# A mixing and gated feed-forward kernel: unit kinds in a table, priorities by tile, and two operations on GpSimd from one copy

## The chip, the cores and the metric

The kernel runs on one core of a Trainium2 chip. The metric is the device time of one execution in microseconds (us); lower is better. A profile is one execution recorded by the hardware profiler; its span goes from the first to the last instruction.

## The reference

```python
X = np.fft.fft(x, axis=1)              # x: 8 x 3008 x 256, float32
X = np.fft.fft(X, axis=2)
x = X.real.reshape(24064, 256)
g = x @ w_gate                         # 256 x 1536
silu = g * (1.0 / (1.0 + np.exp(-g)))
val = x @ w_val                        # 256 x 1536
out = (silu * val) @ w_out             # 1536 x 256
```

A real two-dimensional transform of eight sequences is followed by a gated feed-forward block over all 24064 tokens.

## The kernel before

**Symmetry.** The real part of the transform of a real sequence at position k and at the mirrored position is P + Q and P - Q, with an even part P and an odd part Q. So the kernel computes P and Q for half of the positions (12032 columns and 8 of their own) and gets two tokens from every column: a plus token and a minus (mirrored) token. The transform over the 256 features is put into the weights: `Wp` and `Wq` are the gate (index 0) and value (index 1) weights times cosine and sine tables, and `Wm` is `Wq` with the sign turned and doubled, so that adding `Wm` times Q to a finished P + Q in PSUM makes P - Q.

**Tiles and units.** The columns are cut into 24 tiles, of 512 columns but for tiles 0 and 3 (480) and 23 (320, and the 8 last columns). The 1536 hidden features are cut into 12 blocks f of 128. A unit is one pair (tile, f), 288 in all, 12 to a tile. A unit makes the hidden values `hp` (plus) and `hm` (minus) of its block; when a tile is done, `OWork` (L1188) multiplies them by `Wo`, 12 matmuls of 256 columns to each block of 128 tokens, with `psO` as target, one eviction `ev` on ScalarE (L1220) to two blocks, and stores on SP's queue (L1226). These 96 output matmuls of a tile are spread over the next tile's units.

**Kinds of units.** A plain unit adds P and Q parts of the gate in PSUM (`g`, L974, reached through `mm`), takes silu on ScalarE into `sp` (L1072), adds `Wm` to get the minus gate and takes silu of that into `sv` (L1144): three gate matmuls. The value has two: after the first, the even part is kept in `es`, and after the second the plus value stands in `v`; the mirrored value is twice `es` minus `v`, made by VectorE into `sv` (`mirror_value`, L1158). VectorE makes `hp` = `sp` x `v` (`product_p`, L1168), GpSimd makes `hm` for two units at once from `sv` (`product_m`, L1165). Variations:
- whole units (tiles 0 to 2, `whole_a` and `whole_b`): three matmuls each for gate and value, no `es`;
- seeded units (`seeded`, L957): ScalarE writes the first row's share of the value into PSUM beforehand (`seed_op`, L1046), and `es` is a plain copy on ScalarE (L1095) in place of a VectorE operation (L1097);
- gate-split units (`gate_split`, L967): two gate matmuls in place of three; VectorE keeps the even gate `sg` (L1076) and makes the mirrored gate (`mirror_gate`, L1136); the silus are L1141 and L1144;
- units on GpSimd (`on_pool`, L962): ScalarE copies `v` to `sg` (L1174), and GpSimd makes `hp` from it (`product_g`, L1177).

Which unit is which follows from lists (`SPLIT_1` to `GATE_END`, L944 to L952), one for two alternating tiles (3 to 20) and one for tiles 21 to 23.

**Transforms.** GpSimd folds the loaded x rows (`fold_step`), and a transform on TensorE (`transform_op`, two for each of eight sequences, even and odd parts apart) makes P and Q columns that VectorE puts together (L1387) in tiles from the pool `pq`, five pairs. A part of the folded rows goes to `St` from the pool `st` (three buffers) by copies on SP's queue (`spread_op`, L1339). Row 0 of Q is spread over all partitions by two DMAs on SP's queue to each tile (`br`, L1512, and `bc`, L1520).

**Order.** After a start that is written out by hand, every operation is entered in a planner, `Sched`, with its engine, a duration by formula, what it reads and writes, and the buffers that it needs. `add` (L794) gives it a place `at`: the sum of PE's planned durations so far plus a shift by its kind (`SH_ROW` to `SH_PUT`, L748 to L770). `run` (L825) then picks on each engine, among the operations whose place is at most a window (`WINDOW`, L779) behind the first one's, the one that can start first by the plan; a buffer is handed out in the order of the entries (`ready`, L851). SP's window is 6 us. The operations are issued in that order, and each engine and queue then runs its own in order, with semaphores between them.

Once, ScalarE scales the value half of `Wm` by -0.5 (L1568, at unit `FIRST + 2` = 38), after which seeded units can use it. The weights of feature blocks 4 to 11 land late; the planner has their arrival as entries with a due time (L1542 to L1544), 0 us for the first and 6 us for the second group, gate and value alike. Their products are `weight_op` (L1418).

## Time and profile before

| What | us |
|---|---|
| runs of the kernel (three) | 604.84, 605.88, 608.5; median 605.88 |
| the profiled execution: its time | 605.58 |
| its span, first to last instruction | 603.8 |
| first PE instruction | 1.02 |
| last output matmuls on PE | 592.34 to 600.3 |
| mean granted TensorE clock (share) | 0.999 |
| busy in the span: PE, DVE, ACT, POOL | 593.0, 578.4, 555.6, 485.4 |

How to read it: the busy time of an engine is the time that is covered by its instructions' records. Records of neighbouring instructions overlap, on PE by nearly half of a matmul's length, on DVE and ACT by 0.08 to 0.16 us. So the time that one instruction takes from its engine is the distance from its start to the next one's, which the timeline shows. DVE is VectorE, ACT is ScalarE, POOL is GpSimd, SP issues the DMAs; L974 is line 974 of the kernel.

### The profile page before, as it was taken

Reading aid. Unit: us, or ns where it says so; the run is one execution under the profiler, and the core shown is the slowest. Engines: PE = TensorE matmul, PEld = TensorE weight load, DVE = VectorE, ACT = ScalarE, POOL = GpSimd, SP = SyncE. Lnnn points to the kernel's source line nnn. Section 1 sums busy time; section 2 is a strip of 40 time slices with the busy share of each in tenths; the row PEclk is TensorE's granted clock in tenths of the full one; section 3 lists DMA queues with packets and bytes.
Section 4 is the critical chain, followed back from the end, with each engine's and each line's share of the span. In section 5 each row is a group of like instructions: output and inputs, shape, how many; then the busy total and the mean of one; then the engine's idle time right before and its main releaser. Section 6 shows DMA issues by size and latency. Waiting matters only on the chain.

```text
span 603.8 us, 12560 instructions
## 1 busy us (share of the span) xinstructions
PE 593.0 (98%) x4010; PEld 394.2 (65%) x4067; DVE 578.4 (96%) x1076; ACT 555.6 (92%) x1069; POOL 485.4 (80%) x450
## 2 busy tenths in 40 slices
PE   8999999999999999999999999999999999999997
PEld 6546666666666666666666666667666666666676
DVE  8999999999999999999999999999999999999992
ACT  7688668999999999999999999999999999989984
POOL 8857998999799999987897798987796445549673
PEclk9999999999999999999999999999999999999999
DMA  9965347245515524463262113144221211111212
GB/s 227 138 134 136 106 118 185 89 132 139 153 45 106 143 72 125 120 158 92 59 158 67 54 52 91 54 104 119 62 62 35 63 46 55 45 54 45 60 53 80
DMA packets 51054, 57.91 MB, mean 96 GB/s; under 512 B 7254, under 2 KB 38170, under 8 KB 50988
## 3 DMA queue, kind: packets, MB, share of 16 engines
q1 hardware_dynamic: 47334, 53.97, 33.2%
q0 software_dynamic: 3216, 2.36, 2.8%
q10 hardware_dynamic: 438, 0.77, 0.5%
q8 instruction: 32, 0.52, 0.4%
q14 instruction: 34, 0.28, 0.2%
HBM read 29.43 MB, written 24.65 MB: 90 GB/s over the span
## 4 chain that ended last, share of the span: by engine, by line
PE 90%; POOL 3%; issue 2%; DMA 2%; DVE 2%; ACT 2%; ACTq 0%; DVEq 0%; POOLq 0%
PE o L1214 39%; PE g L974 24%; PE v L974 20%; PE g L1370 2%; PE o L1370 2%; DMA XA<-in_moe_w_val_dram 2%; PE o L299 1%; PE v L1214 1%; POOL hm L1165 1%; POOL EOA L493 1%; ACT sv L1144 1%; PE g L599 0%; DVE sv L1158 0%; DVE hp L1168 0%; ACT sp L1072 0%
## 5 line engine op out<-in xcount | busy, mean ns | idle before, releaser
L1165 POOL TENSOR_TENSOR hm<-sv 128x1024 bf16<-128x1024 f32 (+2 forms) x135 | 251.3, 1862 | 83.7 <-ACT sv L1144 29.8
L1158 DVE SCALAR_TENSOR_TENSOR sv<-es,v 128x512 f32<-128x512 f32 (+2 forms) x270 | 180.5, 670 | 6.7 <-PE v L974 5.7
L1168 DVE TENSOR_TENSOR hp<-sp,v 128x512 bf16<-128x512 f32 (+2 forms) x246 | 165.0, 671 | 0.2 <-ACT sp L1141 0.2
L1214 PE MATMUL o<-Wo,hm 128*128 128x256 bf16 (+1 forms) x1128 | 163.9, 273 | 0.5
L1214 PE MATMUL o<-Wo,hp 128*128 128x256 bf16 (+1 forms) x1104 | 160.5, 272 | 0.6
L1214 PEld LDWEIGHTS <-hm 128*128 128x128 bf16 (+2 forms) x1140 | 111.9, 98 | 59.5 <-issue 0.7
L1214 PEld LDWEIGHTS <-hp 128*128 128x128 bf16 (+2 forms) x1140 | 111.9, 98 | 57.3 <-issue 1.0
L1144 ACT ACTIVATE sv<-g 128x512 f32<-128x512 f32 (+2 forms) x182 | 120.0, 677 | 4.3 <-POOL hm L1165 1.9
L1072 ACT ACTIVATE sp<-g 128x512 f32<-128x512 f32 (+2 forms) x182 | 113.5, 627 | 4.5 <-PE g L974 2.5
L1046 ACT ACTIVATE v<-bc,w 128x512 f32<-128x512 bf16 (+2 forms) x147 | 108.9, 741 | 1.1 <-DVE hp L1168 0.8
L974 PE MATMUL v<-Pt,Wp 128*128 128x512 bf16 (+2 forms) x287 | 106.6, 374 | 0.5 <-DVE hp L1168 0.2
L974 PE MATMUL g<-Pt,Wp 128*128 128x512 bf16 (+2 forms) x281 | 105.2, 374 | 0.8 <-ACT sv L1144 0.2
L1095 ACT COPY es<-v 128x512 f32<-128x512 f32 (+2 forms) x147 | 92.5, 631 | 0.1
L974 PE MATMUL g<-Qt,Wq 128*128 128x512 bf16 (+2 forms) x251 | 92.4, 374 | 0.2
L1097 DVE SCALAR_TENSOR_TENSOR es<-bc,w,v 128x512 f32<-128x512 bf16 (+2 forms) x123 | 89.2, 726 | 2.9 <-PE v L974 1.4
L974 PE MATMUL g<-Qt,Wm 128*128 128x512 bf16 (+2 forms) x196 | 73.3, 374 | 0.3
L974 PEld LDWEIGHTS <-Wp 128*128 128x128 bf16 x576 | 56.2, 98 | 26.0 <-issue 0.8
L1076 DVE SCALAR_TENSOR_TENSOR sg<-bc,w,g 128x512 f32<-128x512 bf16 (+2 forms) x88 | 64.3, 730 | 0.2
L1144 ACT ACTIVATE sv<-sg 128x512 f32<-128x512 f32 (+2 forms) x88 | 63.1, 720 | 0.3 <-DVE sg L1136 0.3
L1220 ACT COPY ev<-o 128x512 f32<-128x512 f32 x89 | 55.9, 628 | 8.0 <-PE o L1214 8.0
L974 PE MATMUL v<-Qt,Wm 128*128 128x512 bf16 (+2 forms) x163 | 61.2, 375 | 0.3
L1141 ACT ACTIVATE sp<-g 128x512 f32<-128x512 f32 (+2 forms) x88 | 55.9, 636 | 4.8 <-DVE sg L1136 4.5
(198 smaller groups left out, 740.0 us busy)
## 6 DMA issues: line engine op xcount, KB each, us to landing
out_dram<-ev SPq DMA_DIRECT2D x96, 128.0 KB
XA<-in_x_dram SPq DMA_DIRECT2D x30, 256.0 KB
XA<-in_x_dram SPq DMA_DIRECT2D x112, 64.0 KB
XC<-in_x_dram SPq DMA_DIRECT2D x30, 120.0 KB
XC<-in_x_dram SPq DMA_DIRECT2D x105, 32.0 KB
bc<-br SPq DMA_DIRECT2D x19, 128.0 KB
St<-Fc SPq DMA_DIRECT2D x12, 128.5 KB
out_dram<-ev SPq DMA_DIRECT2D x12, 120.0 KB
```

The lines of the kernel that those rows point to most:

```text
L974: nc.tensor.matmul(ps[:, :n], Wt[:, gv, fs], src[:, :n], start=start, stop=stop, skip_group_check=True)
L1046: nc.scalar.activation(T_[kv][:, :w], bc[t][:, :w], AF.Copy, scale=w0[:, 1, f:f + 1])
L1072: nc.scalar.activation(T_[ksp][:, :w], T_[kg][:, :w], AF.Silu)
L1076: nc.vector.scalar_tensor_tensor(T_[keg][:, :w], bc[t][:, :w], w0[:, 0, f:f + 1], T_[kg][:, :w], op0=Alu.mult, op1=Alu.add)
L1095: nc.scalar.copy(T_[kes][:, :w], T_[kv][:, :w])
L1097: nc.vector.scalar_tensor_tensor(T_[kes][:, :w], bc[t][:, :w], w0[:, 1, f:f + 1], T_[kv][:, :w], op0=Alu.mult, op1=Alu.add)
L1141: nc.scalar.activation(T_[ksp][:, :wp], T_[kg][:, :wp], AF.Silu)
L1144: nc.scalar.activation(sv()[:, f % 2, w - 1::-1, 1], T_[kgm if by_dve else kg][:, :w], AF.Silu)
L1158: nc.vector.scalar_tensor_tensor(sv()[:, f % 2, w - 1::-1, 0], T_[kes][:, :w], 2.0, T_[kv][:, :w], op0=Alu.mult, op1=Alu.subtract)
L1165: nc.gpsimd.tensor_tensor(hts_(t)[1][:, f - 1:f + 1, :w], sv()[:, :, :w, 1], sv()[:, :, :w, 0], op=Alu.mult)
L1168: nc.vector.tensor_tensor(hts_(t)[0][:, f, :wp], T_[ksp][:, :wp], T_[kv][:, :wp], op=Alu.mult)
L1214: nc.tensor.matmul(st["ps"][:n, j, :], hts[t][minus][:, f, c:c + n], Wo[:, f, :], start=(f == 0), stop=(f == nF - 1))
```

## The change

- The lists of kinds become a table `KINDS`, one character to a unit: w for whole, or a hexadecimal digit, 1 for seeded, 2 for gate-split, and 4 or 8 for GpSimd. 4 is `hp` on GpSimd as before. 8 is new: from one copy of `v` (now in a buffer of its own, `pp`, two of them) GpSimd makes both `hp` and the mirrored value (`mirror_g`), for which the copy to `es` carries a scale of 2.
- The copy to `es` of all seeded units is an activation with a constant scale of 1.0 or 2.0 instead of a copy.
- The shifts become a table `SHIFT` by kind of operation with other values, and a table `BIAS` of some 330 entries adds to them by tile. The windows of PE, ACT, DVE and POOL are 9.75, 7.5, 11.5 and 8.5 instead of 8.5, 6.0, 8.5 and 9.
- The value weights' arrival is entered 3 us later than the gate weights'; `whole_b`'s value product and the rescaling of `Wm` are entered as readers of `Wm`'s parts. The rescaling comes at unit 37.
- The pools `st` and `pq` have two and four buffers instead of three and five.
- Some planned durations change a little; `AHEAD` and `WP_ACT` are new, at values (1 and empty) that leave the old rule in force. Two start units of folds change by one (`A1_AT`, `C2_AT`).

```diff
-    stp = ctx.enter_context(tc.tile_pool(name="st", bufs=3))
-    pqp = ctx.enter_context(tc.tile_pool(name="pq", bufs=5))
+    stp = ctx.enter_context(tc.tile_pool(name="st", bufs=2))
+    pqp = ctx.enter_context(tc.tile_pool(name="pq", bufs=4))
...
+    ppp = Slots("vb", 2)
...
+    RESCALE = 37
+    WP_ACT = ()
...
-    A1_AT = 17
-    C2_AT = 34
+    A1_AT = 16
+    C2_AT = 33
...
-    SH_ROW = 0.15
+    SHIFT = {
+        "ROW": -0.15,
+        "SEED": 2.85,
+        "EG": 3.95,
+        "SP": 2.15,
+        "ES": 0.75,
+        "GM": -3.25,
+        "SM": 4.3,
+        "VM": 3.8,
+        "VAL": -1.1,
+        "HP": 5,
+        "VG": -3.25,
+        "HG": 4.15,
+        "HM": 1.45,
+        "EV": 2.25,
+        "FOLD": 1.3,
+        "OD": -0.95,
+        "PUT": -2.8,
+    }
+    BIAS = {
+        (7, 'EG'): 0.6,
+        (14, 'ROW'): -0.15,
+        (16, 'VAL'): -1.5,
...
+    }
-    W_PE = 8.5
-    W_ACT = 6.0
-    W_DVE = 8.5
-    W_POOL = 9
-    SH_SEED = 2.75
-    SH_EG = 3.25
-    SH_SP = 1.55
-    SH_ES = 2.85
-    SH_GM = -4
-    SH_SM = 3.25
-    SH_VM = 4
-    SH_VAL = 0.0
-    SH_HP = 4
-    SH_HM = 1.05
-    SH_EV = 2.6
-    SH_FOLD = 1.45
-    SH_OD = -3.75
-    SH_PUT = -4
+    W_PE = 9.75
+    W_ACT = 7.5
+    W_DVE = 11.5
+    W_POOL = 8.5
+    AHEAD = 1
...
-            o.at = self.clock + shift
+            o.at = self.clock + (SHIFT[shift] + BIAS.get((self.tile, shift), 0.0) if isinstance(shift, str) else shift)
...
-                    if queue[p][0] != w_ or not free[p]:
+                    if not free[p] or queue[p][0] != w_ and (p not in SLOTS or len(free[p]) < 2 or w_ not in queue[p][:AHEAD]):
...
-    SEED = (1, 2, 3, 4, 5, 6, 8, 11, 13, 14, 15, 16, 17, 21, 23)
-    SEED_END = (4, 5, 7, 10)
-    POOL = (16,)
-    POOL_END = (0, 6, 7, 9, 10)
-    GATE = (0, 2, 4, 5, 7, 14, 15, 16)
-    GATE_END = (0, 4, 7, 9)
+    KINDS = (
+        "wwwwwwwwwwww",
+        "0000000000ww",
+        "202020ww02ww",
+        "013371000101",
+        "213133121001",
+        "013371000101",
+        "213133121001",
+        "013371001101",
+        "213331121001",
+        "013371000101",
+        "213133121001",
+        "013371000101",
+        "213133101201",
+        "013371000101",
+        "213133121001",
+        "013371000111",
+        "213133121001",
+        "013371000101",
+        "213133121001",
+        "013371000101",
+        "211130339021",
+        "610134572610",
+        "141001469230",
+        "712160733213",
+    )
...
-                nc.scalar.copy(T_[kes][:, :w], T_[kv][:, :w])
+                nc.scalar.activation(T_[kes][:, :w], T_[kv][:, :w], AF.Copy, scale=2.0 if on_pool(u) > 1 else 1.0)
...
+        def mirror_g():
+            nc.gpsimd.tensor_tensor(sv()[:, f % 2, w - 1::-1, 0], T_[kes][:, :w], pair_of(u)[:, :w], op=Alu.subtract)
...
         if on_pool(u):
-            S.add("ACT", act_us(wp) - 0.015, value, r=[kv], w=[kval], new=[kval[0]], shift=SH_VAL)
-            S.add("POOL", 0.15 + 2.12e-3 * wp, product_g, r=[ksp, kval], w=[(("h", t), ("p", f))], new=[("h", t)], shift=0.5)
+            S.add("ACT", act_us(wp) + 0.02, value, r=[kv], w=[kval], new=[kval[0]], shift="VAL")
+            if both:
+                S.add("POOL", 0.18 + 2.16e-3 * w, mirror_g, r=[kes, kval], w=[kvm], new=[ksv], shift="VG")
+            S.add("POOL", 0.18 + 2.16e-3 * wp, product_g, r=[ksp, kval], w=[(("h", t), ("p", f))], new=[("h", t)], shift="HG")
...
-            S.add("DMA", 0.01, lambda: None, w=[(("W",), (fc, gv))], lat=at)
+            S.add("DMA", 0.01, lambda: None, w=[(("W",), (fc, gv))], lat=at + 3 * gv)
...
-        if i == FIRST + 2:
+        if i == RESCALE:
             S.add("ACT", 1.3, lambda: nc.scalar.activation(Wm[:, 1], Wm[:, 1], AF.Copy, scale=-0.5),
-                  w=[(("Wm",), 1)])
+                  r=[(("Wm",), (fc, 1)) for fc in range(3)], w=[(("Wm",), 1)])
```

## The prediction

> **What bounds the kernel now.** I read first the busy shares and the 40 slices, then the chain of work that ended last, then the groups by shape, then PE's timeline and its waits, then the stages.

> ```profile
> PE 593.0 (98%) x4010; PEld 394.2 (65%) x4067; DVE 578.4 (96%) x1076; ACT 555.6 (92%) x1069; POOL 485.4 (80%) x450
> ...
> PE   8999999999999999999999999999999999999997
> ...
> DVE  8999999999999999999999999999999999999992
> ACT  7688668999999999999999999999999999989984
> POOL 8857998999799999987897798987796445549673
> ```
> ```profile
> PE 90%; POOL 3%; issue 2%; DMA 2%; DVE 2%; ACT 2%; ACTq 0%; DVEq 0%; POOLq 0%
> ```

> Four engines are nearly full, so busy shares alone decide nothing; the chain says PE. How full PE really is can be read from the distance between starts in its timeline: a 512-column matmul is followed after 0.21 or 0.22 us, whatever its modelled length of 0.38.

> ```profile
> 32.02 0.37 PE L974 MATMUL g<-Pt,Wp 128*128 128x480 bf16 x1
> 32.23 0.37 PE L974 MATMUL g<-Qt,Wq 128*128 128x480 bf16 x1
> 33.10 0.60 PE L1418 MATMUL o<-XA,CD 128*128 128x512 bf16 x2 [0.51 <-DMA XA<-in_moe_w_val_dram]
> ...
> 49.17 0.38 PE L974 MATMUL g<-Qt,Wq 128*128 128x512 bf16 x1
> 49.38 0.38 PE L974 MATMUL v<-Pt,Wp 128*128 128x512 bf16 x1
> 49.60 0.38 PE L974 MATMUL g<-Qt,Wm 128*128 128x512 bf16 x1
> ```

> I took every distance between PE starts and subtracted the usual one for its width (0.216 us at 512 columns, 0.203 at 480, 0.137 at 320 to 328, 0.109 at 256). Excesses of exactly one or two 512-column matmuls are matmuls that the trace did not record (the groups hold 1129 of the 1185 that the table of kinds demands). What remains is PE's idle time: 5.3 us before 25 us, 2.3 from 25 to 50 (0.84 and 0.67 of it in front of two weight products, 0.62 beside the 24 one-column matmuls), and only 2.9 us from 50 us to the end. So PE sets the time from 50 us on, and little is to be had from order alone.

> DVE is next. By the same distances it works 492 of the 500 us between 75 and 575; ACT has more room, and POOL has it only after 450 us:

> ```profile
> 225.00:250.00 25.00, 24.89 (x167) 16.31 (x167) 24.96 (x43) 25.00 (x49) 24.52 (x24) 1.00 0.45 125
> ...
> 475.00:500.00 25.00, 24.84 (x171) 16.52 (x172) 25.00 (x52) 24.43 (x48) 13.62 (x8) 1.00 0.16 49
> ```

> **The change, part by part.** The sum is made against the profiled execution's own 605.58 us (span 603.8 and 1.78 around it); the median of the three runs is 605.88, 0.30 above it.

> Prices are distances between starts at 512 columns: DVE 0.60 (sv L1158, hp L1168, sg L1136) and 0.66 (es L1097, sg L1076); ACT 0.47 (sp), 0.51 or 0.55 (sv), 0.605 (seed, L1046), 0.46 (es, sg and ev copies); POOL 1.85 for a pair's hm, 1.23 for an hp. The durations behind them:

> ```profile
> L1158 DVE SCALAR_TENSOR_TENSOR sv<-es,v 128x512 f32<-128x512 f32 x246 | 166.9, 680 | 4.7 <-PE v L974 3.7 <-POOL hm L1165 0.7
> ...
> L1072 ACT ACTIVATE sp<-g 128x512 f32<-128x512 f32 x165 | 104.6, 637 | 3.9 <-PE g L974 2.5 <-DVE hp L1168 0.6 <-POOL hp L1177 0.3
> L1046 ACT ACTIVATE v<-bc,w 128x512 f32<-128x512 bf16 x136 | 101.9, 749 | 1.1 <-DVE hp L1168 0.8
> ...
> L1095 ACT COPY es<-v 128x512 f32<-128x512 f32 x136 | 86.7, 639 | 0.1
> ...
> L1177 POOL TENSOR_TENSOR hp<-sp,sg 128x512 bf16<-128x512 f32 x18 | 23.0, 1280 | 7.2 <-ACT sg L1174 5.3 <-DVE es L1097 1.3 <-POOL hm L1165 0.6
> ```

> *Table of kinds.* Written out unit by unit, the old rules give the same digits as the new table in all tiles but 7, 8, 12, 15 and 20 to 23; 8 and 12 only exchange places. The engines' work per tile, old to new, with 96 output products and four evictions in it and without the transforms:
> tile 7 and tile 15: PE 22.8 to 22.8, ACT 21.6 to 22.6, DVE 20.8 to 20.1;
> tile 20: PE 22.4 to 22.4, ACT 22.3 to 22.7, DVE 23.2 to 22.0, POOL 11.1 to 13.6;
> tile 21: PE 22.6 to 22.4, ACT 20.3 to 22.4, DVE 21.6 to 21.6;
> tile 22: PE 22.6 to 22.8, ACT 20.3 to 20.8, DVE 21.6 to 19.7;
> tile 23 (328 columns): PE 18.3 to 17.7, ACT 14.9 to 17.4, DVE 14.9 to 17.4, POOL 11.4 to 9.8.
> Over tiles 3 to 23 PE goes from 469.6 to 469.1, ACT from 450 to 458, DVE from 454 to 452, POOL from 257 to 258. On the path lies PE alone: tile 21 saves one 512-column matmul, tile 22 spends it, tile 23 has four more gate-split units, 4 x 0.137 = **-0.55 us**. ACT's 8 us lie beside PE; without that cover they are the slow rival below.

> *Product and mirrored value on POOL* (two units, 20/8 and 22/8). DVE loses sv and hp, 2 x 0.60 each; ACT gains a copy of 0.46; POOL gains two operations. The new subtraction, reversed and with a stride of two, has no row; the nearest are hp, 1.23, and half of the pair's hm, 0.93. I take 1.23, the hp row having one unit's shape; at 0.93 POOL is only freer. Behind it on POOL waits the pair's hm, and behind that the output products of the next tile, which begin only after the tile's last unit, two units (some 4 us) on, and with hp's half; POOL idles 11 of 25 us there. On the path 0. [...]

> *The seeded units' copy* turns from COPY into an ACTIVATE with a constant scale, in all 156 seeded units. No row has that from PSUM: the bounds are the sp row (637, against 639 of the COPY: nothing) and the seed (749: 0.11 more, 17 us on ACT). I take nothing, as the sp row has the same operands and no scale per partition. [...]

> *Weights' arrival.* The value weights are put 3 us later in the planner, so their product no longer stands in PE's queue before they land; other matmuls go first. The stall at 32.2 us was 33.10 - 32.23 - 0.20 = 0.67. Bounds: nothing gained, or 1.51 with the gate weights' stall of 0.84, whose due time is unchanged. I take **-0.67**; late next would be the copies behind it, which the row product at 36 us reads.

> *Rescaling of Wm* one unit earlier, same 1.48 us on ACT; ACT's busy time there is 17.9 of 25 us: 0. *AHEAD = 1* leaves the test as it was, and WP_ACT is empty: 0.

> *Buffers.* Stacks 3 to 2: at 369 us SP copies two stacks in a row; the second must now wait for the transform that reads the older one, seen at 393.7 to 395.9 (at 239 us: until 252.4). SP works in order, so behind the waiting copies stand stores whose place is over 6 us later in the plan, the next x loads (391 us) and rows (396 us). Evictions end some 6 us apart and have three buffers: those of about 379, 384 and 390 fit, the next comes at 397.7. Cost 0, bound +2 (its eviction late by the flood of stores). P and Q from 5 to 4 pairs: a transform writes at most three tiles ahead beside the one in use, four in all, and the oldest was freed four units (8 us) before: 0.

> *Priorities by tile.* They reorder all five queues; the trace can't show it. Bounds: all 2.9 us of idle after 50 us gone, or as much again or more. I count as gone only the bubbles between 457 and 590 us, where units change kind and DVE is relieved: 0.77 in sum, **-0.77**.

> Sum: -0.55 - 0.67 - 0.77 = -2.0; 605.58 - 2.0 = 603.6, and with the 0.30 of the median **603.9 us**. The least possible is all idle after 25 us gone but the 0.62: -0.55 - 1.7 - 2.9 = -5.2, 600.7.

> **Rivals.**
> *It shows nothing:* the reordering makes as many bubbles as it removes, and only PE's 0.55 remains or not even that: 605 to 608. For it: only 2.9 us were there. Chance 0.20.

> *ACT becomes the bound* in tiles 7, 15, 20, 21 and 23, where its work now equals PE's. Against: from 225 to 250 us ACT was busy 25.00 of 25 and PE did not idle. For: elsewhere it idled, 22.29 of 25 at 525 to 550. With its 3.9% of idle between 75 and 575 as unavoidable, the five tiles cost 0.7 + 0.7 + 1.2 + 0.9 + 0.4 = 3.9, 607.8; with 8% it is 1.6 + 1.6 + 2.1 + 1.8 + 1.1 = 8.2, **612**, slower by over 1%; that is the point from which it decides. A dear scaled copy gives the same: ACT's sum passes PE's at (469.1 - 457.9)/156 = 0.072 us each, and at 0.11 it stands 6 above, 610 or more with idle. Chance 0.15 for both.

> *SP blocks* (evictions stand still until 396): if one buffer less covers than I count, PE waits one eviction interval, 6 us, at 390: 610. Against: three buffers, two more in PSUM. Chance 0.04.

> *Faster by over 1%*, under 599.8: beyond the floor of 600.7; only if the start, before the planned part, gets shorter too. Chance 0.03.

> **How the numbers follow.** Forecast 0.58, nothing 0.20, ACT 0.15, SP 0.04, much faster 0.03. One per cent, 6.1 us, is about what a measurement of this kernel can tell from no change. Faster by that 0.03; slower 0.17 (ACT's tail and half of SP's, with the chance that new bubbles exceed 6 us); same 0.80. The range 601 to 609 holds the first two cases, the runs' own scatter of 604.84 to 608.5, and ACT's mild form.

> **What would show it.** PE's group of L974 has four narrow matmuls less; no wait of o L1418 for w_val; es ACTIVATE about 640 ns; POOL's subtraction near 1280 ns; St copies in two pairs, the second at about 252 and 395 us, with no PE idle at 390. Wrong it is if PE's idle after 50 us exceeds 5 us, if ACT idles under 2% while PE idles in tiles 7, 15, 20 or 21, or if es takes over 710.

## The result and the profile after

The changed kernel takes 607.42 us in the median of 22 executions (606.10 to 611.17), the kernel before 605.31 beside it (22 executions, 604.81 to 608.50): 1.0038 times as long, 95% interval 1.0024 to 1.0052. Measured again it came to 607.30 against 605.47, 1.0034 (1.0015 to 1.0053). The forecast was 603.9: the time went up by 2 us where 2 us less were forecast.

First the busy shares and the 40 slices of the first profiled execution (610.03 us, span 608.3), with the chain's shares:

```profile
PE 594.6 (98%) x4007; PEld 393.8 (65%) x4063; DVE 578.4 (95%) x1075; ACT 563.1 (93%) x1085; POOL 486.1 (80%) x450
...
PE   8899999999999999999999999999999999999997
...
DVE  8978999999999999999999999999999999998993
ACT  7677778999999999999999999999999999999994
POOL 8847897999799998996998888976986454567772
PEclk9989999999999999999999999999999999999999
...
PE 83%; DVE 6%; DMA 4%; ACT 3%; issue 2%; POOL 2%; SPq 1%; ACTq 0%; DVEq 0%; POOLq 0%
```

ACT's busy time went from 555.6 to 563.1 us and DVE's and POOL's stayed, as the table of kinds said. PE's share of the chain fell from 90 to 83%: 2% more went to DMA and 4% to DVE, so there are new waits. The groups behind the prices, by shape:

```profile
L1537 DVE SCALAR_TENSOR_TENSOR sv<-es,v 128x512 f32<-128x512 f32 x244 | 167.1, 689 | 4.1 <-PE v L1334 3.3 <-POOL hm L1545 0.2
...
L1407 ACT ACTIVATE v<-bc,w 128x512 f32<-128x512 bf16 x141 | 104.8, 748 | 2.3 <-DVE hp L1548 1.5 <-DMA bc<-br 0.3
...
L1469 ACT ACTIVATE es<-v 128x512 f32<-128x512 f32 x141 | 90.5, 646 | 1.1 <-PE v L1334 0.6
...
L1554 POOL TENSOR_TENSOR hp<-sp,pp 128x512 bf16<-128x512 f32 x18 | 23.0, 1280 | 6.7 <-ACT pp L1551 5.3 <-DVE es L1471 1.4
...
L1557 POOL TENSOR_TENSOR sv<-es,pp 128x512 f32<-128x512 f32 x2 | 2.6, 1280 | 0.0
```

The scaled copy es has 646 ns (639 before), the new subtraction on POOL 1280, the duration of hp: neither new operation got dearer than was taken. The 689 ns of sv on VectorE (680 before) is no mark of the change, as b_fold, an edit of the kernel before, has 687. One entry is new, the seeds' wait for `bc<-br`, the rows spread over the partitions.

PE's own timeline shows the start of this execution:

```profile
28.64 0.37 PE L1334 MATMUL v<-Qt,Wm 128*128 128x480 bf16 x1
31.86 0.87 PE L1800 MATMUL o<-XA,CD 128*128 128x512 bf16 x2 [2.86 <-DMA XA<-in_moe_w_gate_dram]
32.52 0.61 PE L1334 MATMUL v<-Pt,Wp 128*128 128x480 bf16 x1
32.92 0.61 PE L1334 MATMUL v<-Qt,Wq 128*128 128x480 bf16 x1
```

The gate weights landed at 31.81 us (30.09 in the trace of before), PE stood for 3.0 us, and then its matmuls followed each other after 0.40 us rather than 0.20: the granted clock was a half for 3.4 us. I first took this for the change's doing, and it isn't: of 32 executions of the changed kernel 6 have a mean granted clock of 0.997 or less and lie at 609.7 to 611.2, of the 133 of the kernel before whose clock is on record 18 have it and lie at 607.7 to 609.8, both some 3 us above the rest. A second profiled execution of the same kernel (608.59, span 606.8, clock 1.000) is nearer to the usual one. PE's idle time by the distances between its starts, in us (the 5.0 holds 1.6 that the half clock cost):

| stretch | before | after, first | after, second |
|---|---|---|---|
| to 25 us | 5.3 | 4.8 | 4.0 |
| 25 to 50 | 2.3 | 5.0 | 1.5 |
| 50 to 75 | 0.5 | 0.0 | 2.2 |
| 75 to 400 | 1.5 | 1.7 | 1.6 |
| 400 to 425 | 0.0 | 1.1 | 1.7 |
| 425 to the last matmul | 1.0 | 1.1 | 1.1 |
| last matmul to the span's end | 3.5 | 4.3 | 4.4 |

With 0.55 us less of matmuls this makes 1.9 of the 3.0 us by which the second span is longer; the other 1.0 was found at no place. The trace of before records 4010 matmuls where another of the same matmuls (b_fold) records 4067, and beside those that are missing idle time can't be told. Three places stand out: 50 to 75 us, 400 to 425 us and the tail. In the middle stages PE and ACT look as they did, and GpSimd is a little freer (22.27 us busy in the first window against 24.52); two windows of the first execution:

```profile
225.00:250.00 25.00, 24.84 (x167) 16.45 (x169) 24.23 (x40) 24.83 (x49) 22.27 (x20) 1.00 0.44 125
475.00:500.00 25.00, 24.84 (x171) 16.58 (x173) 24.93 (x52) 24.39 (x47) 13.08 (x8) 1.00 0.16 48
```

**At 410 us.** SP's queue, the kernel before and then the changed one (second execution):

```profile
375.69 15.69 SPq L1226 DMA_DIRECT2D out_dram<-ev  x9
391.48 2.02 SPq L144 DMA_DIRECT2D XA<-in_x_dram  x6
396.38 0.53 SPq L1512 DMA_DIRECT2D br<-Qt  x1
398.32 1.31 SPq L1226 DMA_DIRECT2D out_dram<-ev  x3
399.73 0.56 SPq L1520 DMA_DIRECT2D bc<-br  x1
```
```profile
379.75 0.81 SPq L1608 DMA_DIRECT2D out_dram<-ev  x2
396.85 1.79 SPq L1721 DMA_DIRECT2D St<-Fc  x2
398.73 2.69 SPq L1608 DMA_DIRECT2D out_dram<-ev  x6
401.52 0.53 SPq L1900 DMA_DIRECT2D br<-Qt  x1
402.17 1.45 SPq L1608 DMA_DIRECT2D out_dram<-ev  x3
404.04 1.71 SPq L144 DMA_DIRECT2D XA<-in_x_dram  x4
405.80 0.58 SPq L1908 DMA_DIRECT2D bc<-br  x1
```

Before, SP issues stores all through; after, it issues nothing from 380.6 to 396.9, and its own waits in that window say why:

```profile
SPq L1721 <- PE v L1334: 16.6, 1, 16.6
```

The second pair of stack copies (St) waits for PE to read the older stack, and behind it stand nine stores with br among them, four loads and then bc, which is issued 6.1 us later than before. ACT's seed waits for bc, and PE for the seed and what hangs on it:

```profile
410.09 0.69 ACT L1407 ACTIVATE v<-bc,w 128x512 f32<-128x512 bf16 x1 [0.89 <-DMA bc<-br]
```
```profile
410.83 0.38 PE L1334 MATMUL v<-Pt,Wp 128*128 128x512 bf16 x1 [0.57 <-ACT v L1407]
411.59 0.38 PE L1334 MATMUL g<-Qt,Wq 128*128 128x512 bf16 x1 [0.39 <-DVE sg L1450]
412.79 0.28 PE L1596 MATMUL o<-Wo,hp 128*128 128x256 bf16 x1 [0.28 <-DVE hp L1548]
```

**At 58 us.** POOL's timeline before, then that of the second execution, and then PE's:

```profile
47.36 2.35 POOL L174 TENSOR_TENSOR SDf<-XC 128x1020 f32<-128x1020 f32 x1 [9.33 <-DMA XA<-in_x_dram]
...
53.07 1.90 POOL L1165 TENSOR_TENSOR hm<-sv 128x1024 bf16<-128x1024 f32 x1 [1.11 <-ACT sv L1144]
```
```profile
48.76 2.36 POOL L174 TENSOR_TENSOR SDf<-XC 128x1020 f32<-128x1020 f32 x1 [11.60 <-DMA XA<-in_x_dram]
...
57.33 1.90 POOL L1545 TENSOR_TENSOR hm<-sv 128x1024 bf16<-128x1024 f32 x1
```
```profile
57.91 0.38 PE L1334 MATMUL g<-Qt,Wm 128*128 128x512 bf16 x1
59.94 0.38 PE L1334 MATMUL g<-Pt,Wp 128*128 128x512 bf16 x1 [1.65 <-ACT sv L1521]
```

POOL folds the second block as soon as its rows are there, at 48.8 us (47.4 in the trace of before), and hm, on which ACT's sv and then PE wait, comes behind the whole fold; before, it stood in the middle of it, at 53.1.

**The tail.** The end of the chain, before and then after:

```profile
598.89 1.44 PE g L1214 x12
600.33 0.03 ACTq L1223
600.36 0.04 issue
600.40 0.37 ACT ev L1223
```
```profile
600.25 2.79 DMA out_dram<-ev
603.04 0.02 issue
...
603.19 0.37 ACT ev L1605
```

Before, the last eviction follows the last matmul (ended at 600.32). After, the last matmul ends at 602.38, and the last eviction waits until 603.19 for an older eviction's store, which gives its buffer back.

### The profile page after: what moved, and what is told of

Same layout as the page of the kernel before. It is cut to its first block, busy times and chain, and to the rows that moved or that the text cites. A ratio compares the mean times of both kernels' runs of the same rounds, so it can differ in the third digit from the quotient of the medians.

```text
span 608.3 us, 12557 instructions
## 1 busy us (share of the span) xinstructions
PE 594.6 (98%) x4007; PEld 393.8 (65%) x4063; DVE 578.4 (95%) x1075; ACT 563.1 (93%) x1085; POOL 486.1 (80%) x450
## 4 chain that ended last, share of the span: by engine, by line
PE 83%; DVE 6%; DMA 4%; ACT 3%; issue 2%; POOL 2%; SPq 1%; ACTq 0%; DVEq 0%; POOLq 0%
PE o L1596 36%; PE g L1334 23%; PE v L1334 19%; PE g L1752 2%; PE o L1752 2%; DMA XA<-in_moe_w_gate_dram 2%; DVE sv L1537 1%; DVE hp L1548 1%; DMA XA<-in_x_dram 1%; ACT sv L1521 1%; DVE sg L1514 1%; DVE sg L1450 1%; POOL EOA L493 1%; DMA bc<-br 1%; ACT sp L1446 1%
## 5 line engine op out<-in xcount | busy, mean ns | idle before, releaser
L1548 DVE TENSOR_TENSOR hp<-sp,v 128x512 bf16<-128x512 f32 (+2 forms) x248 | 167.7, 679 | 3.0 <-PE v L1334 1.8
L1521 ACT ACTIVATE sv<-g 128x512 f32<-128x512 f32 (+2 forms) x178 | 117.9, 684 | 0.8 <-PE g L1334 0.3
L1407 ACT ACTIVATE v<-bc,w 128x512 f32<-128x512 bf16 (+2 forms) x156 | 114.2, 736 | 2.3 <-DVE hp L1548 1.5
L1469 ACT ACTIVATE es<-v 128x512 f32<-128x512 f32 (+2 forms) x156 | 98.5, 636 | 1.1 <-PE v L1334 0.6
L1471 DVE SCALAR_TENSOR_TENSOR es<-bc,w,v 128x512 f32<-128x512 bf16 (+2 forms) x114 | 84.3, 740 | 3.6 <-PE g L1334 1.3
L1450 DVE SCALAR_TENSOR_TENSOR sg<-bc,w,g 128x512 f32<-128x512 bf16 (+2 forms) x92 | 67.2, 730 | 1.4 <-PE g L1334 1.2
L1521 ACT ACTIVATE sv<-sg 128x512 f32<-128x512 f32 (+2 forms) x92 | 64.8, 708 | 0.4 <-DVE sg L1514 0.3
L1334 PE MATMUL v<-Qt,Wm 128*128 128x512 bf16 (+2 forms) x169 | 63.1, 374 | 0.2
L1514 DVE SCALAR_TENSOR_TENSOR sg<-sg,g 128x512 f32<-128x512 f32 (+2 forms) x92 | 61.5, 669 | 0.4 <-PE g L1334 0.4
```

Source lines behind the costliest of these rows:

```text
L1334: nc.tensor.matmul(ps[:, :n], Wt[:, gv, fs], src[:, :n], start=start, stop=stop, skip_group_check=True)
L1407: nc.scalar.activation(T_[kv][:, :w], bc[t][:, :w], AF.Copy, scale=w0[:, 1, f:f + 1])
L1450: nc.vector.scalar_tensor_tensor(T_[keg][:, :w], bc[t][:, :w], w0[:, 0, f:f + 1], T_[kg][:, :w], op0=Alu.mult, op1=Alu.add)
L1469: nc.scalar.activation(T_[kes][:, :w], T_[kv][:, :w], AF.Copy, scale=2.0 if on_pool(u) > 1 else 1.0)
L1471: nc.vector.scalar_tensor_tensor(T_[kes][:, :w], bc[t][:, :w], w0[:, 1, f:f + 1], T_[kv][:, :w], op0=Alu.mult, op1=Alu.add)
L1514: nc.vector.scalar_tensor_tensor(T_[kgm][:, :w], T_[keg][:, :w], 2.0, T_[kg][:, :w], op0=Alu.mult, op1=Alu.subtract)
```

## The experiments

The theory at first (A): the change loses at three places, the start, the late rows, the last eviction. Its rival (B): many small bubbles from the new priorities.

**Parts of the change put into the kernel before: the weights' due time (b_val), the buffers (b_bufs).**

```
b_val:   lat=at   ->  lat=at + 3 * gv
b_bufs:  st 3 -> 2 and pq 5 -> 4, in the pools and in BUFS
```

> The kernel before, with one part of the change alone: the value weights are entered 3 us later, everything else old. It moves one value matmul (0.20 us) ahead of the value weights' product at 32 us and touches little else. Theory A (the loss comes from three places: the gate weights' wait at 28.6 us, rows late behind SP at 412 us, the last eviction): the gate weights' product is not moved by this part, so its wait stays and follows the landing (0.84 us in the profile before); gain at most 0.2 to 0.7, so 0.999 to 1.000 of before. Theory B (the order by the new priorities makes many small bubbles everywhere): this part is free of them, 1.000. If it gives 1.002 or more, this part itself is at fault and both fall.

> The kernel before, with two stack buffers and four P and Q pairs instead of three and five, everything else old. Theory A: SP waits with the second stack's copies at about 370 until the transform at 394 to 396 us has read the old stack; the stores, x loads and rows behind it come late, so that the row copy of the tile that begins near 410 us lands after it is wanted: PE idles about 1 us near 410 us, time 1.001 to 1.003 of before. Theory B: the wait is hidden by three eviction buffers, as my prediction had it: 1.000, and no bubble over 0.3 us between 400 and 425 us beyond those of before.

b_val: 605.42 us against 605.71, ratio 0.9996 (0.9978 to 1.0014). PE still waited 0.63 and 0.30 us for the two weights. The due time alone shows no gain; the interval, some 1.1 us to either side, can't tell the forecast 0.67 from nothing.

b_bufs: 606.19, ratio 1.0009 (0.9993 to 1.0024). The stand of SP is there in full, by SP's own waits between 376 and 412 us:

```profile
SPq L1339 <- PE v L974: 15.3, 1, 15.3
```

PE's matmuls come in the same order as before, one by one, and there the stand cost PE 0.34 us at 400 to 425 us, not more. So the buffers make the stand, and the order decides how much of it reaches PE.

**The second stack copy entered later (a_late), the gate weights' due time later (a_gate), in the changed kernel.**

```
a_late, in the loop over the units:
-            spread_op(spread_at[i])
+            b_ = spread_at[i]
+            spread_op(b_, (0,) if b_ > 2 else (0, 1))
+            if b_ > 2:
+                late_at[slot[(b_ - 1, 1)] + 3] = b_
+        if i in late_at:
+            spread_op(late_at[i], (1,))
a_gate:
-    for fc, at in ((1, 0.0), (2, 6.0)):
+    for fc, at in ((1, 0.0), (2, 9.0)):
```

> The changed kernel, but the second stack's copies of two sequence pairs are entered only after the transform that frees their buffer (two units later than it), so SP no longer stands still 16 us at 383 to 399 us. Theory A: the bubbles of 0.55 and 0.44 us at 412 to 414 us go; about 1.1 us less than the changed kernel, 1.002 of before instead of 1.0038. Theory B: no difference from the changed kernel beyond 0.3 us (1.0035 to 1.004).

> The changed kernel, but the second group's weights are entered at 9 us (gate) and 12 us (value) instead of 6 and 9, so that eight more matmuls (1.6 us) stand ahead of the gate product at 28.6 us. Theory A: the wait of 3.0 us there shrinks by 1.6 us, and with it the half clock of 31.9 to 35.4 us (1.2 us) goes: no execution near 611 us any more; in executions where the weights land early (30.1 us as in the profile before) the gain is 1 us or less. Median 1.5 to 2.5 us below the changed kernel, 1.000 to 1.001 of before. Theory B: the start is not where typical executions lose; 1.003 to 1.004 as before this edit.

a_late: 606.39, ratio 1.0008 (0.9991 to 1.0025). SP stands 2.2 us for the copies and no longer 16.6:

```profile
SPq L1724 <- PE v L1334: 2.2, 1, 2.2
```

Idle at 400 to 425 us is 0.08, with PE's matmuls in the changed kernel's order, one by one. Of the change's loss 1.0 us is gone by the medians (607.42 to 606.39) and 1.8 by the ratios (1.0038 to 1.0008). So in this order the stand is the cause of this place.

a_gate: 611.58, ratio 1.0088 (1.0064 to 1.0111). Theory A's step for the start fell: PE's wait for the gate weights went, and yet the kernel became 4 us slower. PE idled 8.6 us after 75 us (4.4 in the second trace of the changed kernel), spread from 225 to 575 us. A plan shifted at its beginning comes out in another order to its end: laid beside the changed kernel's sequence of matmuls, less than half of a_gate's (0.46) stands in the same order. That the priorities no longer fit this order is argued, not shown. It spoke for B's point that the order is fragile.

**The same kernel again (after_again), and the 58-us place (a_late_hm, b_fold).** Theory C took the start for a matter of the single execution and put the losses at 58 us (hm behind the fold on GpSimd), at 410 us and behind the last matmul.

```
a_late_hm = a_late and:   (1, 'FOLD'): 1.1  ->  3.0
b_fold (before):          shift=SH_FOLD  ->  SH_FOLD - 3 * (what == ("C", 1))
```

> The changed kernel once more, nothing edited: is its first profile the usual one? Theory A (start, rows at 412 us, last eviction): the start's gate wait of 3.0 us and the 3.4 us of half clock come again in most executions, mean clock 0.997. Theory C (start is a lottery that both kernels play; what the change costs lies at 58, 412 and behind 600 us): with the clock at 1.000 the start's waits sum to under 1.5 us, and instead PE idles 1.3 to 1.9 us between 57 and 64 us in front of g<-Pt,Wp, 1.0 to 1.2 us at 410 to 414 us, and the tail behind the last matmul is 0.6 to 1.0 us longer than before's 3.5; the time is then 606.5 to 608.

> The changed kernel with the second stack copy entered later (as in the run that did that alone) and with one priority of tile 1 changed, that of the fold (1.1 to 3.0), so that on GpSimd one hm goes ahead of five fold steps near 55 us; nothing else moves. Theory C: the 1.50 and 0.39 us in front of g<-Pt,Wp at 58 and 63 us go, the time is 604.3 to 605.0 (606.4 less 1.5 to 1.9), at or just under the kernel before. Theory B (many small bubbles): the idle comes back elsewhere, 606.0 to 606.5.

> The kernel before, with only the order of GpSimd near 55 us taken from the changed one: five fold steps ahead of one hm (the fold's shift for that block is 3 less). Theory C: PE idles 1.3 to 1.9 us more between 57 and 64 us when the start runs without its long wait, and the time is 606.5 to 607.3. Rival: later slack takes it up, as POOL has idle time there: no difference, under 0.3 us.

after_again agreed with C in every place and was above it in size: 2.2 us between 57 and 64 us and 1.7 at 410 to 414. a_late_hm: 606.03, ratio 1.0004 (0.9986 to 1.0022); in its profile the 58-us place was empty, but so were its rows early (fold at 47.2). b_fold: 604.99, ratio 1.0004 (0.9982 to 1.0026); hm stood behind the whole fold, ended at 58.2, and PE idled 0.2 us. The order on GpSimd showed no cost by itself; that part of C fell.

Set side by side, the traces show what goes with the idle time: where the fold begins at 46.5 to 47.8 us (seven traces, of either kernel and its edits) PE idles 0 to 1.2 us between 50 and 75, where it begins at 48.2 to 49.3 it idles 1.6 to 2.2, in whichever order. The clearest pair is a_late_hm and a_hm_tail (below), whose instructions are the same up to the last eviction: the fold began at 47.2 and at 49.3 us, and PE idled 0.0 and 2.2. The exceptions are the three executions that had lost 2 to 3 us at the start already. That is theory D: the second block's rows land late.

**More load on the transfers (b_load).** The edit is b_bufs and, behind the output weights' load:

```
+    extra = const.tile([P, 2, T], BF16, name="extra")
+    nc.gpsimd.dma_start(out=extra, in_=moe_w_gate...[:, :, 0:T])
```

> The kernel before, with the fewer buffers of the run that had these alone (stacks 2, pq 4), and one more load of 256 KB behind the output weights, into a buffer that nothing reads; at the 130 to 140 GB/s of this stretch that is 2 us of the transfers. Theory D (the 1.5 to 2.2 us in front of g<-Pt,Wp near 58 us come when the second block's rows land late, whatever the order on GpSimd): the fold on GpSimd begins at 48.5 to 50 us rather than at 46.5 to 47.8, PE idles 1.0 us or more between 57 and 66 us, the time is 606.5 to 608. Rival (the order on GpSimd or the priorities make it): idle there under 0.5 us, 605.7 to 606.3.

The median is 607.38 (606.22 to 607.95) against 605.63, the ratio by the comparison of all runs 1.0011 (0.9995 to 1.0028). Six of the 29 executions beside it, and none of its 12, have the clock of 0.997 or less; without these six the medians are 607.38 and 605.44. The profile is plain:

```profile
50.02 2.36 POOL L174 TENSOR_TENSOR SDf<-XC 128x1020 f32<-128x1020 f32 x1 [11.61 <-DMA XA<-in_x_dram]
...
54.58 1.90 POOL L1167 TENSOR_TENSOR hm<-sv 128x1024 bf16<-128x1024 f32 x1
...
61.86 3.75 POOL L1167 TENSOR_TENSOR hm<-sv 128x1024 bf16<-128x1024 f32 x2
```

The fold begins at 50.0, one hm goes ahead in the middle of it, the next two wait for its end, and PE idles 1.7 us at 62.7. D holds in this trace: late rows cost PE these 1.7 us, also in the old order. What stays open is why the rows came after 48.2 us in 8 of the 11 traces of the changed kernel and its edits and in only one (b_kinds) of the five of the kernel before without the extra load, SP's and GpSimd's orders being alike up to there. So it is not shown that the change makes this loss.

**The tail (a_hm_tail).** a_late_hm, with the last eviction in another buffer and its store on another queue:

```
+            if st["last"]:
+                st["ev"] = ev = ppp.tile([P, T], F32, name="pp").rearrange("p (j d) -> p j d", j=2)
...
+            eng = nc.scalar if st["last"] else nc.sync
```

> The same kernel, with the very last eviction written into a pair buffer, which is free by then, and stored by the DMA queue of ScalarE rather than SP's. Theory C: the last eviction no longer waits 0.7 to 1.0 us for the store of an older one, the tail behind the last matmul goes from 4.4 to 3.4 to 3.8 us, and the time is 0.5 to 1.0 under the kernel without this edit: 603.5 to 604.4, under the kernel before. If the tail is set by the stores themselves and not by the buffer: no difference.

606.23, ratio 1.0008 (0.9987 to 1.0028). The last eviction now follows the last matmul at once (601.21, 601.24), but the span ends 4.3 us behind it, as before the edit: the last stores, bunched at 601.5 to 602.3, set the end. The buffer wait was real and paid for nothing. With the tail in SP's hands, what counts is that the last three evictions start 2.2 and 1.6 us apart (a_late), where before it was 3.1 and 1.4: the stores of three come out of one queue in less time. All 17 traces agree: the five with 3.1 us between the third-last and the second-last eviction end 3.5 us behind the last matmul, the twelve with 1.4 to 2.2 us end 4.0 to 4.5 behind it. But no run changes this spacing alone, so the reason is argued.

**Kinds and priorities apart (b_kinds, a_kinds, a_nobias).**

```
b_kinds (before): tiles 20 to 23 by "211130335021", "610134572610", "141001465230", "712160733213"
a_kinds (after):  tiles 20 to 23 by "213133121001", "600031470650" three times
a_nobias (after): BIAS = {}
```

> The kernel before, with only the new unit kinds of tiles 20 to 23 (the two units of kind 9 as kind 5: GpSimd makes their product, DVE their mirrored value), everything else as it was. If the prediction's PE step holds by itself: matmuls of 0.55 us less in tile 23 and no new bubble, 604.7 to 605.1. Theory B (the kinds and the order go together): a new order of the last 100 us gives idle of 0.5 us or more on PE after 500 us, or a last eviction that waits as in the changed kernel (last store issued 1.8 us after the last matmul rather than 1.0), 605.6 to 606.5.

> The changed kernel, with the unit kinds of tiles 20 to 23 as they were before. Theory C: the matmuls are 0.55 us more and the tail stays or falls by up to 0.8 us: 607.0 to 607.9 where the changed kernel has 607.3. If the new kinds of the last tiles are what makes it slow: 605.8 to 606.5.

> The changed kernel without its table of priorities by tile (the shifts by kind of work stay). Prediction's step on the priorities: they close bubbles, so that without them PE idles more after 75 us than the 2.7 us that remain in the changed kernel once the 410-us place is mended; 608.5 to 613. Rival: they are fitted to a timing that the chip does not keep, and do nothing on the chip: 606.5 to 608, or less than the changed kernel if the 410-us place is of their making.

b_kinds: 611.69, ratio 1.0106 (1.0077 to 1.0135), 6 us and not under 1. PE idled 6.8 us between 550 us and the end, at places of this kind:

```profile
551.82 0.38 PE L979 MATMUL v<-Pt,Wp 128*128 128x512 bf16 x1 [0.62 <-ACT v L1051]
...
555.41 0.38 PE L979 MATMUL g<-Pt,Wp 128*128 128x512 bf16 x1 [0.47 <-ACT sp L1146]
...
582.59 0.30 PE L979 MATMUL v<-Qt,Wm 128*128 128x328 bf16 x1 [0.60 <-ACT es L1100]
```

The new kinds give ACT more work, and in the old order PE waits for ACT. a_kinds: 608.85, ratio 1.0051 (1.0033 to 1.0068), slower too, and above both expectations. a_nobias: 609.06, ratio 1.0050 (1.0031 to 1.0070), with 3.4 us of idle behind 525 us rather than 0.8. Kinds and priorities are one thing: either alone is worse than both or neither. The 410-us place was empty in a_nobias (0.03), which made me suspect the priorities there.

**The table of priorities split (a_bias20, a_bias_no15), and two edits joined (a_late20).** a_bias20 keeps the entries of tiles 20 to 23 alone, a_bias_no15 drops those of tiles 14 to 16, a_late20 is a_bias20 with a_late's edit.

> The changed kernel with the priorities by tile kept for tiles 20 to 23 alone. Theory: the entries up to tile 19 make the 410-us place and buy nothing measurable, those from 20 on buy the 3 us that came up behind 525 us without the table. Then idle at 400 to 425 us under 0.3 us, idle behind 525 us under 0.9, last store issued 1.8 us after the last matmul as before, 605.3 to 606.4. If the entries up to tile 19 do close bubbles: idle between 75 and 400 us of 2.5 us or more rather than 1.7, 607 to 608.

> The changed kernel without the priorities of tiles 14 to 16, all others kept. Theory: these entries move the second stack copy ahead of the rows in SP's queue; without them the 1.1 to 1.7 us at 410 us go, and the time is 605.7 to 606.6. If the place comes of two stack buffers rather than three alone: 1.0 us or more stay there, 607 to 607.6. If the later order falls apart instead, as it did where the start was shifted: over 608.

> The changed kernel with two edits that each took about 1 us: the second stack copy is entered later, and the priorities by tile are kept for tiles 20 to 23 alone. If the two add up: SP does not stand still between 380 and 396 us, idle at 400 to 425 us under 0.2 us, 604.9 to 605.5, that is 0.9985 to 1.0 of the kernel before. If the tail behind the last matmul and the late rows near 58 us weigh as in the changed kernel: 605.5 to 606.2, no gain on the kernel before.

a_bias_no15: 606.53, ratio 1.0019 (1.0002 to 1.0035); 1.1 us of idle stayed at 400 to 425, SP stood from 379 to 395. The suspicion fell for these tiles; what keeps the place empty in a_nobias, where SP stands 16.8 us as well, stays open. SP stands 15 to 17 us in every one of the eight kernels here that have two stacks and the early second copy, and at most 3 us for the copies in the eight others.

a_bias20: 606.06, ratio 1.0001 (0.9988 to 1.0013), with 0.7 us of idle left at 400 to 425 and 2.0 at 50 to 75. So the entries up to tile 19 buy nothing, and the kernel is 1.2 us better off without them by the medians (2.2 by the ratios), as much as by a_late; those from 20 on are the ones that the kinds need.

a_late20: 605.83 against 605.71, ratio 1.0003 (0.9983 to 1.0022). SP does not stand, 400 to 425 us has 0.04, the last matmul ends at 599.0 us (600.3 in the trace of before), and the span at 603.5, 4.5 us on: the tail takes back what PE saved. The two edits bring the kernel level with the one before; none of the runs is measurably under it.

## Why the prediction was wrong

**Buffers, taken at 0 with a bound of 2: the step that failed.** Place, time and reason of SP's wait were forecast (393.7 to 395.9; it came at 396.9), and PE did not idle at 390. The step named "the next x loads (391 us) and rows (396 us)" as queued behind the waiting copy, and then counted only the evictions and their three buffers. The rows were what mattered: br and bc are a chain through the same queue behind nine stores, and the seed needs them at 410 us. It cost 1.1 to 1.7 us of idle in the two traces, and a_late got 1.0 us back by the medians, 1.8 by the ratios. The bound of 2 holds this by luck, as it was priced for a late eviction. The step also took the buffers by themselves: in the old order their stand costs 0.34 us (b_bufs), and only the new order of the same change lets more of it reach PE.

**Priorities, taken at -0.77: the second step that failed.** The bubbles from 425 us on sum to 1.0 before and 1.1 after, those from 75 to 400 to 1.5 and 1.6 to 1.7: nothing gained. The table closes bubbles, 3.4 down to 0.8 us behind 525 us, but those are ones that the new kinds open, and its entries up to tile 19 cost 1.2 us by the medians (a_bias20). The forecast counted as gone bubbles of the old order that the new one has again.

**Weights' arrival, taken at -0.67.** By itself it shows no gain (b_val, which can't resolve it). In the second trace PE loses 0.41 and 0.12 us in front of the two weight products, where it lost 0.84 and 0.67, but both weights also landed 1.6 us earlier there (28.51 and 31.49 us), so the due time's part can't be told. The start idles 2.1 us less up to 50 us in all, and PE gives 1.7 back at 58, where the next limit is the landing of the second block's rows, which no step named.

**The tail, not in the sum.** 0.9 us more behind the last matmul, for which no term stood. The last stores set the end there; why they come later is argued above, not shown.

**What held.** PE's matmuls: in two traces that recorded nearly all of them, b_fold and after_again, their usual distances sum to 586.59 and 586.05, 0.54 less. The subtraction on POOL at 1280 ns, as taken; nothing waited for it. The scaled copy at 646 ns, at the lower of its two bounds. ACT not the bound: between 550 and 575 us of the second execution it is busy 24.74 of 25 and PE 25.00; yet b_kinds shows that this rival was no invention, since in the old order the same kinds (but for two units) gave 611.7, near its 612. The range of "It shows nothing", 605 to 608, holds the 607.4, but partly by luck: its reason, as many bubbles made as removed, fits the stretch from 75 to 400 us and that from 425 us on, and the losses came at 410 us, at 58 us and in the tail, which it did not name. The sign of error that the prediction set itself, more than 5 us of PE idle after 50 us, shows in the second trace, 2.2 + 1.6 + 1.7 + 1.1 = 6.6, and not in the first, 0.0 + 1.7 + 1.1 + 1.1 = 3.9.

## What to carry to other kernels

When a buffer is taken away from something that an in-order DMA queue fills, list everything that stands behind the waiting transfer on that queue, chains of two transfers above all, and ask when each is needed; here bc came 6.1 us later behind a wait of 16.6 us on SP's queue, and the three eviction buffers that the prediction counted said nothing on that. A table of work and a table of priorities that were fitted together can't be judged or taken over one without the other (611.7 and 609.1 against 607.3). Before a stall in one profile is explained, profile the same kernel a second time: the half clock behind the largest stall of the first trace here shows in the mean clock of 6 of 32 executions of the changed kernel and of 18 of 133 of the one before.

## What the runs showed of the hardware

Whether a wait of PE was followed by half clock did not go by the wait's length alone. In the first trace a wait of 2.86 us in front of 31.86 us was followed by 3.41 us at half clock, in a_kinds one of 1.99 us in front of 31.71 likewise, while in b_kinds one of 2.73 us in front of 32.22 left the clock at 1.00.

While a transfer waited for a semaphore, SP's queue stood with it: 16.6 us in the second execution of the changed kernel, in which nothing else left the queue, and 15 to 17 us in each of the eight kernels with that wait.
